# Whole-tile loads of K and V in a decode attention kernel: K tiles alternate between two overlapping places

## The chip, the core and the metric

The kernel runs on one core of a Trainium2 chip. The metric is the device time of one execution in microseconds. The profile's span, from the first to the last instruction, is 1.4 us shorter: 200.9 us in an execution of 202.28 us.

## What is computed

One token goes through a transformer layer: attention over a cache of 4096 positions with 32 heads of 128, then a gated feed-forward part. All tensors are bfloat16.

```
x  = A_x                                   # 1 x 640
q  = layernorm(x) @ wq                     # 640 -> 32 heads x 128
p  = softmax(q . k_cache / sqrt(128))      # 32 heads, 4096 positions each
o  = p @ v_cache                           # 32 x 128
h  = x + o @ wo                            # 4096 -> 640
g, u = layernorm(h) @ w_gate, layernorm(h) @ w_up     # 640 -> 1728
out  = h + (gelu(g) * u) @ w_down
```

Each head has its own keys and values, so no cache byte is used twice. K and V are 33.6 MB each; with the weights, 84.2 MB are read in all.

## The kernel before

**Tiles.** The work on the cache runs over four tiles (`j` from 0 to 3, `NG = 4`) of eight heads. A tile of K or V is 8.39 MB: on each of the 128 partitions 256 rows of 128 numbers, 64 KB in one piece of memory. Sixteen partitions share a head.

**Halves and quarters.** `k_all` has 64 KB per partition, one tile of K. It is loaded in two halves of 32 KB (`load_k(j, s)`, `HALF` = 128 rows), each with a landing event of its own. VectorE works on quarters of 64 rows: `mult(j, s, i)` (L393) multiplies quarter `i` of half `s` by the query into `prod[i]`. TensorE sums a product over groups of its 128 numbers by matmuls with the identity (`fold`, L369 and L167, 16 matmuls a quarter) into four PSUM banks. `total(j, s)` (L399) reduces what is left for both quarters of a half to 128 scores per partition, and ScalarE takes the exponential (L401). `block(j, s)` (L406) spreads the 128 probabilities into `p_bd[s]`, a block form that TensorE can multiply with V. There is no maximum subtraction.

**V.** `v_all` has 64 KB per partition, one tile of V, and holds wq before the first tile. `pv(s)` (L381) runs 32 matmuls of `p_bd[s]` with half `s` of V. The first three tiles of V come in one load each, the last in two. The next load of V waits for `pvs[j, 1]`, the end of the second half's matmuls.

**Order.** `Prog` keeps a list of operations for each engine, each with the events that it waits for; an engine works through its list in order. All big loads are issued by SyncE, whose list also runs in order: a load that waits holds up those behind it. VectorE's order for a tile is mult(0,0), mult(0,1), mult(1,0), total(0), mult(1,1), block(0), total(1), block(1). TensorE has a loop over the tiles with the steps f00, f01, f10, f11 (folds), p0, p1 (V matmuls) and h (sum over a head's partitions). In before, p0 waits for `blocks[j, 0]` and p1 for `blocks[j, 1]`. One-element GpSimd memsets of `spare` (L437) serve as a relay: each waits for the second half of V, and p1 waits for the memset.

**K's release.** The load of half `s` of tile `j + 1` waits for `mults[j, s, 1]`, the second product of that half.

**Tail.** After the last tile, wo goes into the first 40 KB of `k_all`, w_down into the 16.25 KB behind it, and w_gate and w_up into `v_all`. The loads of wo wait for the last product of tile 3; w_gate waits for the last V matmul, `pvs[3, 1]`; w_up and w_down are behind it in SyncE's list. TensorE then does the output projection (L486), a layer norm, gate and up (L516) and w_down (L539). Three nops stand on VectorE's list after the product `hm` (`idle("vector", 3)`).

Of the kernel before, what the change touches and what calls it, by code (L numbers as in the profile page):

```python
# [5 lines left out]
FP32 = mybir.dt.float32  # L6
BF16 = mybir.dt.bfloat16
ALU = mybir.AluOpType
ACTF = mybir.ActivationFunctionType
AX = mybir.AxisListType  # L10
# [3 lines left out]
DH = 128  # L14
# [6 lines left out]
NG = 4  # L21
# [158 lines left out]

def bass_sequential_preLN__gqa_block_cached__glu_gated_geglu__decode_kernel(nc, A_x, A_k_cache, A_v_cache, A_wq, A_wo, B_x, B_w_gate, B_w_up, B_w_down, out):
    sb = lambda name, shape, dt: nc.alloc_sbuf_tensor(name, shape, dt)
    k_all = sb("k_all", [128, 2 * 128 * DH], BF16)
    v_all = sb("v_all", [128, 256 * DH], BF16)
    prod = sb("prod", [128, 2, 64, DH], BF16)
    qb = sb("qb", [128, NG, DH], BF16)
    sc = sb("sc", [128, 128], FP32)
    pt = sb("pt", [128, 128], BF16)
    spare = sb("spare", [1, 1], FP32)
    own = sb("own", [128, 4], BF16)  # L190
    own8 = sb("own8", [128, 8], BF16)
    p_bd = sb("p_bd", [128, 2, 128, 8], BF16)
# [36 lines left out]
    ps_f = psum[:, 0:2048]  # L229
# [8 lines left out]
    wo_sb = k_all[:, 0:32 * D].rearrange("p (i n) -> p i n", i=32)  # L238
    tile3 = lambda ap: ap.rearrange("p (g d) -> p g d", d=DH)


    P = Prog(nc)
    V = lambda fn, *d: P.op("vector", fn, *d)
# [8 lines left out]
    mults, pvs = {}, {}  # L252
    landed = {}
    HALF = 128 * DH

    def load_k(j, s):
        src = A_k_cache[0, 8 * j:8 * j + 8, :, :].rearrange("h (p r) d -> (h p) (r d)", p=16)
        landed["K", j, s] = P.dma("sync", k_all[:, HALF * s:HALF * s + HALF], src[:, HALF * s:HALF * s + HALF],
                                  mults.get((j - 1, s, 1)))

    def load_v(j, lo, hi, *after, chan=None):
        src = A_v_cache[0, 8 * j:8 * j + 8, :, :].rearrange("h (p r) d -> (h p) (r d)", p=16)
        ev = P.dma("sync", v_all[:, HALF * lo:HALF * hi], src[:, HALF * lo:HALF * hi], *after, chan=chan)
        for i in range(lo, hi):
            landed["V", j, i] = ev

    load_k(0, 0)
    load_k(0, 1)


    c_xz = GP(lambda e: e.memset(xlnB[:, :, :], 0.0))
# [17 lines left out]
    c_own8 = GP(lambda e: e.affine_select(own8[:, :], own8[:, :], pattern=[[16, 8]], compare_op=ALU.is_ge,  # L289
                                          fill=0.0, base=15, channel_multiplier=-1), own1)  # L290
# [20 lines left out]
    def idle(eng, n):  # L311

        def fn(e):
            for _ in range(n):
                i = e.nop(hint="n", nofuse=True)
            return i
        return P.op(eng, fn)
# [37 lines left out]
    qd = T(q_proj, xl, d_wq)  # L355
    VM = lambda fn, *d: P.op("vector", fn, *d, chan="m")
    VR = lambda fn, *d: P.op("vector", fn, *d, chan="r")
    VB = lambda fn, *d: P.op("vector", fn, *d, chan="b")
    AS = lambda fn, *d: P.op("scalar", fn, *d, chan="s")
    GS = lambda fn, *d: P.op("gpsimd", fn, *d, chan="s")  # L360
    qa = VR(lambda e: e.tensor_copy(qb[:, :, :].rearrange("p g d -> p (g d)"), ps_q), qd)  # L361
    load_v(0, 0, 2, qd, chan="V")


    reds, exps, blocks, evs, folds, seen = {}, {}, {}, {}, {}, {}

    def half(e, i, s, first=True):
        for n in range(8):
# [4 lines left out]
    def fold(e, i):  # L373
        half(e, i, 0)
        return half(e, i, 1, False)

    def pv(e, s):
        vt = tile3(v_all[:, HALF * s:HALF * s + HALF])
        for b in range(32):
            a = 32 * (b % 4)  # L380
            i = e.matmul(ps_o[a:a + 32, :], p_bd[:, s, 4 * b:4 * b + 4, :].rearrange("p g j -> p (g j)"),  # L381
                         vt[:, 4 * b:4 * b + 4, :], start=(s == 0 and b < 4), stop=(s == 1 and b >= 28))
        return i

    def head_sum(e, at):
        for r in range(4):
            i = e.matmul(ps_a[:, bass.ds(at, 8)], po_sb[:, 128 * r:128 * r + 128], hs[:, r, :],  # L387
                         start=(r == 0), stop=(r == 3))
        return i

    def mult(j, s, i):
        kt = tile3(k_all[:, HALF * s:HALF * s + HALF])
        mults[j, s, i] = VM(lambda e: e.tensor_tensor(  # L393
            out=prod[:, i, :, :], in0=kt[:, 64 * i:64 * i + 64, :],
            in1=qb[:, j, :].unsqueeze(1).to_broadcast([128, 64, DH]), op=ALU.mult),
            landed["K", j, s], qa, folds.get((j, 0, i) if s else (j - 1, 1, i)))

    def total(j, s):
        reds[j, s] = VR(lambda e: e.reduce_sum(sc[:, :], ps_f.rearrange("p (g d) -> p g d", d=16), axis=AX.X), folds[j, s, 1],  # L399
                        exps.get((j, 0) if s else (j - 1, 1)))  # L400
        exps[j, s] = AS(lambda e: e.activation(pt[:, :], sc[:, :], ACTF.Exp, bias=zero_t[:, 0:1],  # L401
                                               scale=INV_SQRT_DH, accum_out=RS[:, 2 * j + s:2 * j + s + 1]), reds[j, s], c_eps,
                        blocks.get((j, 0) if s else (j - 1, 1)))

    def block(j, s):
        blocks[j, s] = VB(lambda e: e.tensor_tensor(  # L406
            out=p_bd[:, s, :, :], in0=pt[:, :].unsqueeze(2).to_broadcast([128, 128, 8]),
            in1=own8[:, :].unsqueeze(1).to_broadcast([128, 128, 8]), op=ALU.mult), exps[j, s], c_own8, pvs.get((j - 1, s)))

    T(None, c_idb, c_hs)  # L410
    lp = P.loop("tensor", range(NG), [
# [1 line left out]
        ("f01", lambda e, j: fold(e, 1), lambda j: [mults[j, 0, 1]], True),  # L413
        ("f10", lambda e, j: fold(e, 0), lambda j: [mults[j, 1, 0], reds[j, 0]], True),
        ("f11", lambda e, j: fold(e, 1), lambda j: [mults[j, 1, 1]], True),
        ("p0", lambda e, j: pv(e, 0), lambda j: [blocks[j, 0], landed["V", j, 0]], True),
        ("p1", lambda e, j: pv(e, 1), lambda j: [blocks[j, 1], seen[j]], True),
        ("h", lambda e, j: head_sum(e, j * 8), lambda j: [evs[j]], True)])
    for j in range(NG):
        for s in range(2):  # L420
# [3 lines left out]
    for j in range(NG):  # L424
        mult(j, 0, 0)
        mult(j, 0, 1)
        if j < NG - 1:
            load_k(j + 1, 0)
        mult(j, 1, 0)
        total(j, 0)  # L430
        mult(j, 1, 1)
        if j < NG - 1:
            load_k(j + 1, 1)
        block(j, 0)
        total(j, 1)
        block(j, 1)
        seen[j] = GS(lambda e: e.memset(spare[:, :], 0.0), landed["V", j, 1])  # L437
        if j < NG - 2:
            load_v(j + 1, 0, 2, pvs[j, 1], chan="V")
        elif j == NG - 2:  # L440
            load_v(j + 1, 0, 1, pvs[j, 1], chan="V")
            load_v(j + 1, 1, 2)
        evs[j] = AS(lambda e: e.copy(po_sb[:, :], ps_o), pvs[j, 1])  # L443

    rt = GP(lambda e: e.tensor_tensor(out=RT[:, :, :], in0=RS[:, :].unsqueeze(2).to_broadcast([128, 2 * NG, 8]),
                                     in1=own8[:, :].unsqueeze(1).to_broadcast([128, 2 * NG, 8]), op=ALU.mult), exps[NG - 1, 1])
    def z_sum(e):
        for s in range(2):
# [6 lines left out]
                                      in1=own[:, :].unsqueeze(1).to_broadcast([128, H, 4]), op=ALU.mult), at)  # L455
# [2 lines left out]
    ap = V(lambda e: e.tensor_copy(aP[:, :], ps_z[:, 32:64]), sp)  # L458


    d_wo = [P.dma("sync", wo_sb[:, i:i + 16, :], A_wo[:, :].rearrange("(p i) n -> p i n", i=32)[:, i:i + 16, :], mults[NG - 1, 1, 1])
            for i in (0, 16)]
    wg_sb = v_all[:, 0:5 * DF].rearrange("p (c n) -> p c n", c=5)
    wu_sb = v_all[:, 5 * DF:10 * DF].rearrange("p (c n) -> p c n", c=5)
# [7 lines left out]
    for o in (0, 1, 2, 3, 32, 33, 34, 35):  # L472
        lo = o - o % 32
# [55 lines left out]
    g6 = V(lambda e: e.tensor_mul(gu[:, :], g_t[:, :], t1[:, :]), g8)  # L529
    g9 = V(lambda e: e.tensor_mul(hm[:, :], gu[:, :], ps_u[:, 0:15]), g6, up)  # L530

    idle("vector", 3)

    def down(ms, qs=range(4)):
        def fn(e):
            for m in ms:
                for q in qs:
                    rows, wd = (128, wd_sb[:, m]) if m < 13 else (48, wd_lo[:, m - 13])
                    i = e.matmul(ps_d[32 * q:32 * q + 1, 0:160], hm[0:rows, m:m + 1],  # L539
                                 wd[0:rows, col[q]:col[q] + 160], start=False, stop=(m == 12))  # L540
            return i
        return fn
# [46 lines left out]
```

The softmax here doesn't subtract the row's maximum and nothing guards it: scores larger than these inputs give would overflow.

## Time and profile before

| | |
|---|---|
| time, median of 3 | 202.29 us (202.2 to 202.43) |
| span of the profiled execution | 200.9 us |
| read from HBM | 84.23 MB, 419 GB/s over the span |
| busy: TensorE matmul / VectorE / ScalarE | 115.3 / 103.6 / 9.4 us |
| 16 products of K (L393) | 4.42 us each |
| 8 reductions (L399) | 2.29 us each |
| 8 p_bd (L406) | 1.22 us each |
| TensorE clock granted, mean | 0.795 |

In the page, the row "DMA" gives for each of 40 equal slices of the span the mean busy share of the 16 transfer engines in tenths, and the row below what they moved. A line of the timeline is: start in us, length in us, engine, line, operation, output and inputs, how many, and in square brackets how long the engine stood idle before and what it waited for. "DMA" as a releaser means that a load landed. A line with SPq is SyncE issuing a transfer, not the transfer itself.

### The profile page before, as it was taken

What the parts mean: (1) busy time and instruction counts of PE and PEld (TensorE: products, weight loads), DVE (VectorE), ACT (ScalarE), POOL (GpSimd) and SP (SyncE); (2) the same over time, 40 slices, a digit from 0 to 9 for tenths busy, and PEclk for the clock granted to TensorE, in tenths of its full rate; (3) what the DMA queues carried; (4) which work ended last, traced back from release to release, by engine and by line L of the source; (5) the groups of instructions that cost most, each with busy time, mean ns of one, the idle gap of its engine ahead of it and who ended that gap; (6) DMA issues with size and microseconds to landing.
All of it is one profiled execution on the core that took longest, in us unless ns stands there. A gap on an engine that the chain in (4) does not pass through costs nothing.

```text
span 200.9 us, 2025 instructions
## 1 busy us (share of the span) xinstructions
PE 115.3 (57%) x982; PEld 30.4 (15%) x738; DVE 103.6 (52%) x56; ACT 9.4 (5%) x27; POOL 6.7 (3%) x36
## 2 busy tenths in 40 slices
PE   0108019667094296696605938566088496674675
PEld 0103000000032000001300000023000001474574
DVE  0200197994601969945149799420798965120320
ACT  2100000000001000000100000001000000100100
POOL 6500000000000000000000000000000000000000
PEclk9999856999858559579965899969669879955555
DMA  8999999999899999999999999899999999999992
GB/s 326 449 406 437 431 450 424 417 431 499 385 444 417 424 522 417 417 417 411 417 424 424 489 457 444 378 411 424 424 450 437 431 444 391 432 436 414 423 402 107
DMA packets 3275, 84.31 MB, mean 420 GB/s; under 512 B 387, under 2 KB 582, under 8 KB 966
## 3 DMA queue, kind: packets, MB, share of 16 engines
q1 hardware_dynamic: 3266, 84.23, 97.8%
q8 instruction: 4, 0.07, 0.1%
q14 instruction: 1, 0.01, 0.0%
q10 hardware_dynamic: 4, 0.00, 0.0%
HBM read 84.23 MB, written 0.00 MB: 419 GB/s over the span
## 4 chain that ended last, share of the span: by engine, by line
DMA 66%; DVE 22%; PE 11%; issue 0%; ACT 0%; SPq 0%; DVEq 0%
DMA k_all<-in_A_k_cache_dram 56%; DVE prod L393 18%; DMA v_all<-in_B_w_up_dram 10%; PE psum L167 7%; DVE sc L399 3%; PE psum L516 1%; PE psum L539 1%; PE psum L381 1%; DVE p_bd L406 1%; PE psum L369 1%; SPq L59 0%; ACT pt L401 0%; ACT out_row L555 0%; DVE hm L530 0%; DVEq L114 0%
## 5 line engine op out<-in xcount | busy, mean ns | idle before, releaser
L393 DVE TENSOR_TENSOR prod<-k_all,qb 128x8192 bf16<-128x8192 bf16 x16 | 70.4, 4421 | 38.0 <-DMA k_all<-in_A_k_cache_dram 33.1
L167 PE MATMUL psum<-prod,id_b 128*128 128x512 bf16 x240 | 66.0, 437 | 0.0
L369 PE MATMUL psum<-prod,id_b 128*128 128x512 bf16 x16 | 7.3, 454 | 45.3 <-DVE prod L393 31.5
L381 PE MATMUL psum<-v_all,p_bd 128*32 128x512 bf16 x256 | 19.4, 464 | 14.2 <-DMA v_all<-in_A_v_cache_dram 11.0
L399 DVE TENSOR_REDUCE sc<-psum 128x128 f32<-128x2048 f32 x8 | 18.3, 2288 | 13.3 <-PE psum L167 13.3
L369 PEld LDWEIGHTS psum<-prod,id_b 128*128 128x128 bf16 x16 | 1.6, 99 | 99.8 <-DVE prod L393 59.4
L381 PEld LDWEIGHTS psum<-v_all,p_bd 128*32 128x32 bf16 x256 | 7.5, 114 | 38.5 <-DMA v_all<-in_A_v_cache_dram 21.8
L406 DVE TENSOR_TENSOR p_bd<-pt,own 128x1024 bf16<-128x1024 bf16 x8 | 9.8, 1222 | 2.2 <-ACT pt L401 2.2
L401 ACT ACTIVATE pt<-sc,zero_t 128x128 bf16<-128x128 f32 x8 | 3.2, 402 | 135.9 <-DVE sc L399 135.9
L352 PE MATMUL psum<-v_all,xlnB 128*32 128x512 bf16 x40 | 4.5, 631 | 6.7 <-DMA v_all<-in_A_wq_dram 6.7
L486 PE MATMUL psum<-aP,k_all 128*128 128x1 bf16 x160 | 6.7, 178 | 2.7 <-DMA k_all<-in_A_wo_dram 2.7
L486 PEld LDWEIGHTS psum<-aP,k_all 128*128 128x128 bf16 x160 | 6.6, 131 | 2.8 <-DMA k_all<-in_A_wo_dram 2.8
L516 PE MATMUL psum<-hlnT,v_all 128*128 128x1 bf16 x150 | 5.5, 173 | 1.2 <-DMA v_all<-in_B_w_up_dram 1.2
L387 PE MATMUL psum<-hs,po_sb 128*128 128x8 f32 x32 | 4.2, 258 | 3.2 <-ACT po_sb L443 3.2
L437 POOL MEMSET spare<- 1x1 f32 x4 | 0.4, 88 | 162.8 <-DMA v_all<-in_A_v_cache_dram 162.8
L361 DVE CAST qb<-psum 128x512 bf16<-128x512 f32 x1 | 0.7, 692 | 9.7 <-PE psum L352 9.7
L516 PEld LDWEIGHTS psum<-hlnT,v_all 128*128 128x128 bf16 x150 | 5.3, 120 | 1.8 <-DMA v_all<-in_B_w_up_dram 1.3
L492 DVE COPY hT<-psum 128x5 f32<-128x5 f32 x1 | 0.2, 166 | 9.6 <-PE psum L486 9.6
L387 PEld LDWEIGHTS psum<-hs,po_sb 128*128 128x128 f32 x32 | 3.9, 191 | 5.1 <-issue 5.1
L323 PE MATMUL psum<-one_bf,x_row 1*128 1x1 bf16 x5 | 0.4, 177 | 7.1 <-DMA x_row<-in_A_x_dram 7.1
L326 DVE COPY xx<-psum 128x5 f32<-128x5 f32 x1 | 0.2, 165 | 7.5 <-PE psum L323 7.5
L443 ACT COPY po_sb<-psum 128x512 f32<-128x512 f32 x4 | 2.3, 585 | 22.3 <-PE psum L381 22.3
(71 smaller groups left out, 28.6 us busy)
## 6 DMA issues: line engine op xcount, KB each, us to landing
k_all<-in_A_k_cache_dram SPq DMA_DIRECT2D x8, 4096.0 KB, 29.1
v_all<-in_A_v_cache_dram SPq DMA_DIRECT2D x2, 4096.0 KB, 28.5
v_all<-in_A_wq_dram SPq DMA_DIRECT2D x1, 5120.0 KB, 15.2
k_all<-in_A_wo_dram SPq DMA_DIRECT2D x2, 2560.0 KB, 17.4
v_all<-in_B_w_gate_dram SPq DMA_DIRECT2D x1, 2160.0 KB, 15.0
v_all<-in_B_w_up_dram SPq DMA_DIRECT2D x1, 2160.0 KB, 19.8
k_all<-in_B_w_down_dram SPq DMA_DIRECT2D x1, 800.0 KB, 22.3
k_all<-in_B_w_down_dram SPq DMA_DIRECT2D x1, 640.0 KB, 20.9
```

The costliest lines, as they stand in the source:

```text
L167: built = e.matmul(out, lhsT, rhs, start=start, stop=stop)
L352: i = e.matmul(ps_q[32 * t:32 * t + 32, :], xlnB[:, c, 32 * a:32 * a + 32], wq_j[:, c, t, a, :, :], start=(c == 0 and a == 0), stop=(c == ...
L369: mm = held if n or not first else lambda e, *a, **k: e.matmul(*a, **k)
L381: i = e.matmul(ps_o[a:a + 32, :], p_bd[:, s, 4 * b:4 * b + 4, :].rearrange("p g j -> p (g j)"), vt[:, 4 * b:4 * b + 4, :], start=(s == 0 a ...
L387: i = e.matmul(ps_a[:, bass.ds(at, 8)], po_sb[:, 128 * r:128 * r + 128], hs[:, r, :], start=(r == 0), stop=(r == 3))
L393: mults[j, s, i] = VM(lambda e: e.tensor_tensor(out=prod[:, i, :, :], in0=kt[:, 64 * i:64 * i + 64, :], in1=qb[:, j, :].unsqueeze(1).to_br ...
L399: reds[j, s] = VR(lambda e: e.reduce_sum(sc[:, :], ps_f.rearrange("p (g d) -> p g d", d=16), axis=AX.X), folds[j, s, 1], exps.get((j, 0) i ...
L401: exps[j, s] = AS(lambda e: e.activation(pt[:, :], sc[:, :], ACTF.Exp, bias=zero_t[:, 0:1], scale=INV_SQRT_DH, accum_out=RS[:, 2 * j + s:2 ...
L406: blocks[j, s] = VB(lambda e: e.tensor_tensor(out=p_bd[:, s, :, :], in0=pt[:, :].unsqueeze(2).to_broadcast([128, 128, 8]), in1=own8[:, :]. ...
L443: evs[j] = AS(lambda e: e.copy(po_sb[:, :], ps_o), pvs[j, 1])
L486: r = e.matmul(ps_p[:, c:c + 1], wo_sb[:, i, c::5], aP[:, i:i + 1], start=False, stop=(i == 31), skip_group_check=True)
L516: i = e.matmul(ps[:, m:m + 1], ws, hlnT[:, c:c + 1], start=(c == 0 and m == 0), stop=(c == 4), skip_group_check=True)
```

## The change

K's whole tile comes in one load, and so does V's. `k_all` grows to 80 KB per partition. Even tiles of K lie at 0 to 64 KB, odd tiles at 16 to 80 KB (`K_AT`). The two places overlap in 48 KB, so the next tile can be loaded as soon as three of a tile's four quarters are used, if the one that lies outside the overlap is used last. For this, even tiles use their quarters in the order 2, 3, 1, 0 and odd tiles in the order 0, 1, 2, 3. The next load of K waits for the third product, `mults[j, 1, 0]`.

With the new order, the first pair of an even tile's products belongs to the second half of the positions: `half_of` puts its probabilities into the matching half of `p_bd`, and the second pair, which comes as quarters 1 and 0, is reduced in two instructions that swap them back. Both V steps now wait for the second `block` of the tile, and for the whole V tile; the relay on GpSimd is gone. The loads of wo wait only for tile 3's second product, since wo covers only its first two quarters. The three nops on VectorE near the end are taken out.

The aim is fewer and larger loads, with the next K tile requested once rather than in two steps.

```diff
-    k_all = sb("k_all", [128, 2 * 128 * DH], BF16)
+    k_all = sb("k_all", [128, 320 * DH], BF16)
...
-    def load_k(j, s):
+    K_AT = [0, 64 * DH, 0, 64 * DH]
+
+    def load_k(j):
...
-        landed["K", j, s] = P.dma("sync", k_all[:, HALF * s:HALF * s + HALF], src[:, HALF * s:HALF * s + HALF],
-                                  mults.get((j - 1, s, 1)))
+        landed["K", j] = P.dma("sync", k_all[:, K_AT[j]:K_AT[j] + 2 * HALF], src, mults.get((j - 1, 1, 0)))
...
+    def half_of(j, s):
+        return s if j % 2 else 1 - s
+
     def mult(j, s, i):
-        kt = tile3(k_all[:, HALF * s:HALF * s + HALF])
+        c = (2 * s + i) if j % 2 else (2 + i, 1 - i)[s]
+        kt = tile3(k_all[:, K_AT[j]:K_AT[j] + 2 * HALF])
...
-            out=prod[:, i, :, :], in0=kt[:, 64 * i:64 * i + 64, :],
+            out=prod[:, i, :, :], in0=kt[:, 64 * c:64 * c + 64, :],
...
-            landed["K", j, s], qa, folds.get((j, 0, i) if s else (j - 1, 1, i)))
+            landed["K", j], qa, folds.get((j, 0, i) if s else (j - 1, 1, i)))
...
+        if s and j % 2 == 0:
+            V(lambda e: e.reduce_sum(sc[:, 64:128], g16(0, 1024), axis=AX.X), folds[j, s, 1], free)
+            reds[j, s] = VR(lambda e: e.reduce_sum(sc[:, 0:64], g16(1024, 2048), axis=AX.X))
+        else:
+            reds[j, s] = VR(lambda e: e.reduce_sum(sc[:, :], g16(0, 2048), axis=AX.X), folds[j, s, 1], free)
...
-        ("p0", lambda e, j: pv(e, 0), lambda j: [blocks[j, 0], landed["V", j, 0]], True),
-        ("p1", lambda e, j: pv(e, 1), lambda j: [blocks[j, 1], seen[j]], True),
+        ("p0", lambda e, j: pv(e, 0), lambda j: [blocks[j, 1], landed["V", j]], True),
+        ("p1", lambda e, j: pv(e, 1), lambda j: [], True),
...
         mult(j, 0, 1)
+        mult(j, 1, 0)
         if j < NG - 1:
-            load_k(j + 1, 0)
-        mult(j, 1, 0)
+            load_k(j + 1)
         total(j, 0)
         mult(j, 1, 1)
-        if j < NG - 1:
-            load_k(j + 1, 1)
         block(j, 0)
         total(j, 1)
         block(j, 1)
-        seen[j] = GS(lambda e: e.memset(spare[:, :], 0.0), landed["V", j, 1])
-        if j < NG - 2:
-            load_v(j + 1, 0, 2, pvs[j, 1], chan="V")
-        elif j == NG - 2:
-            load_v(j + 1, 0, 1, pvs[j, 1], chan="V")
-            load_v(j + 1, 1, 2)
+        if j < NG - 1:
+            load_v(j + 1, pvs[j, 1])
...
-    d_wo = [P.dma("sync", wo_sb[:, i:i + 16, :], A_wo[:, :].rearrange("(p i) n -> p i n", i=32)[:, i:i + 16, :], mults[NG - 1, 1, 1])
+    d_wo = [P.dma("sync", wo_sb[:, i:i + 16, :], A_wo[:, :].rearrange("(p i) n -> p i n", i=32)[:, i:i + 16, :], mults[NG - 1, 0, 1])
...
-    idle("vector", 3)
-
```

More of the change, by code (lines that the diff above doesn't have):

```diff
@@ L188, in bass_sequential_preLN__gqa_block_cached__glu_gated_geglu__decode_kernel @@
     pt = sb("pt", [128, 128], BF16)
-    spare = sb("spare", [1, 1], FP32)
     own = sb("own", [128, 4], BF16)
@@ L254, in bass_sequential_preLN__gqa_block_cached__glu_gated_geglu__decode_kernel, with load_v @@
     HALF = 128 * DH
-    def load_k(j, s):
+    K_AT = [0, 64 * DH, 0, 64 * DH]
+    def load_k(j):
         src = A_k_cache[0, 8 * j:8 * j + 8, :, :].rearrange("h (p r) d -> (h p) (r d)", p=16)
-        landed["K", j, s] = P.dma("sync", k_all[:, HALF * s:HALF * s + HALF], src[:, HALF * s:HALF * s + HALF],
-                                  mults.get((j - 1, s, 1)))
-    def load_v(j, lo, hi, *after, chan=None):
+        landed["K", j] = P.dma("sync", k_all[:, K_AT[j]:K_AT[j] + 2 * HALF], src, mults.get((j - 1, 1, 0)))
+    def load_v(j, *after):
         src = A_v_cache[0, 8 * j:8 * j + 8, :, :].rearrange("h (p r) d -> (h p) (r d)", p=16)
[L263 to L268, printed above, removed]
+        landed["V", j] = P.dma("sync", v_all[:, 0:2 * HALF], src, *after, chan="V")
+    load_k(0)
     c_xz = GP(lambda e: e.memset(xlnB[:, :, :], 0.0))
@@ L361, in bass_sequential_preLN__gqa_block_cached__glu_gated_geglu__decode_kernel @@
     qa = VR(lambda e: e.tensor_copy(qb[:, :, :].rearrange("p g d -> p (g d)"), ps_q), qd)
-    load_v(0, 0, 2, qd, chan="V")
-    reds, exps, blocks, evs, folds, seen = {}, {}, {}, {}, {}, {}
+    load_v(0, qd)
+    reds, exps, blocks, evs, folds = {}, {}, {}, {}, {}
     def half(e, i, s, first=True):
@@ L389, in head_sum @@
         return i
+    def half_of(j, s):
+        return s if j % 2 else 1 - s
     def mult(j, s, i):
-        kt = tile3(k_all[:, HALF * s:HALF * s + HALF])
+        c = (2 * s + i) if j % 2 else (2 + i, 1 - i)[s]
+        kt = tile3(k_all[:, K_AT[j]:K_AT[j] + 2 * HALF])
         mults[j, s, i] = VM(lambda e: e.tensor_tensor(
-            out=prod[:, i, :, :], in0=kt[:, 64 * i:64 * i + 64, :],
+            out=prod[:, i, :, :], in0=kt[:, 64 * c:64 * c + 64, :],
             in1=qb[:, j, :].unsqueeze(1).to_broadcast([128, 64, DH]), op=ALU.mult),
-            landed["K", j, s], qa, folds.get((j, 0, i) if s else (j - 1, 1, i)))
+            landed["K", j], qa, folds.get((j, 0, i) if s else (j - 1, 1, i)))
     def total(j, s):
-        reds[j, s] = VR(lambda e: e.reduce_sum(sc[:, :], ps_f.rearrange("p (g d) -> p g d", d=16), axis=AX.X), folds[j, s, 1],
-                        exps.get((j, 0) if s else (j - 1, 1)))
+        free = exps.get((j, 0) if s else (j - 1, 1))
+        g16 = lambda lo, hi: ps_f[:, lo:hi].rearrange("p (g d) -> p g d", d=16)
+        if s and j % 2 == 0:
[3 more added lines that the diff above has]
+            reds[j, s] = VR(lambda e: e.reduce_sum(sc[:, :], g16(0, 2048), axis=AX.X), folds[j, s, 1], free)
         exps[j, s] = AS(lambda e: e.activation(pt[:, :], sc[:, :], ACTF.Exp, bias=zero_t[:, 0:1],
@@ L405, in block @@
     def block(j, s):
+        hf = half_of(j, s)
         blocks[j, s] = VB(lambda e: e.tensor_tensor(
-            out=p_bd[:, s, :, :], in0=pt[:, :].unsqueeze(2).to_broadcast([128, 128, 8]),
-            in1=own8[:, :].unsqueeze(1).to_broadcast([128, 128, 8]), op=ALU.mult), exps[j, s], c_own8, pvs.get((j - 1, s)))
+            out=p_bd[:, hf, :, :], in0=pt[:, :].unsqueeze(2).to_broadcast([128, 128, 8]),
+            in1=own8[:, :].unsqueeze(1).to_broadcast([128, 128, 8]), op=ALU.mult), exps[j, s], c_own8, pvs.get((j - 1, 1)))
     T(None, c_idb, c_hs)
```

## The prediction

> **What bounds the kernel now.** I read the page's DMA row and queue table first, because the kernel reads every byte of the two caches once.
>
> ```profile
> DMA  8999999999899999999999999899999999999992
> GB/s 326 449 406 437 431 450 424 417 431 499 385 444 417 424 522 417 417 417 411 417 424 424 489 457 444 378 411 424 424 450 437 431 444 391 432 436 414 423 402 107
> q1 hardware_dynamic: 3266, 84.23, 97.8%
> ```
>
> The transfer engines are busy from the first slice to the last but one. No compute engine passes 57% of the span. To see whether any gap is left, I take landing times from the timeline. The GpSimd memset of `spare` waits for nothing but a V landing, so its start is that landing:
>
> ```profile
> 54.92 0.09 POOL L437 MEMSET spare<- 1x1 f32 x1 [46.68 <-DMA v_all<-in_A_v_cache_dram]
> 93.70 0.09 POOL L437 MEMSET spare<- 1x1 f32 x1 [38.69 <-DMA v_all<-in_A_v_cache_dram]
> 132.48 0.09 POOL L437 MEMSET spare<- 1x1 f32 x1 [38.69 <-DMA v_all<-in_A_v_cache_dram]
> 171.34 0.09 POOL L437 MEMSET spare<- 1x1 f32 x1 [38.77 <-DMA v_all<-in_A_v_cache_dram]
> ```
>
> Steps of 38.78, 38.78 and 38.86 us, each with one K and one V tile between (16.78 MB): 432.6 GB/s, with no room for a gap. So the loads are an unbroken stream: wq, K0, V0, K1, V1, K2, V2, K3, V3, wo, the small pieces of w_down, w_gate, w_up, w_down.
>
> Next the chain of work that ended last, in order of time (start, length, what), from the last K half on:
>
> ```profile
> 124.58 27.28 DMA k_all<-in_A_k_cache_dram
> 151.85 0.02 issue
> 151.88 4.42 DVE prod L393
> ...
> 171.66 1.94 PE psum L381 x32
> 173.60 0.02 issue
> 173.61 0.34 SPq L59
> 173.95 0.04 issue
> 173.99 19.78 DMA v_all<-in_B_w_up_dram
> 193.77 0.05 issue
> 193.82 2.77 PE psum L516 x75
> ```
>
> The second half of K3 lands at 151.85. The arithmetic on it, up to the last probability-times-V matmul, ends at 173.60; that frees `v_all`, and w_gate and w_up are issued. w_up lands at 193.77 and the end follows 7.1 us later. The chain calls this one transfer of 19.78 us, but wo is still in front of it. The timeline of TensorE has its landing as the wait before the second half of the output projection:
>
> ```profile
> 183.53 3.36 PE L486 MATMUL psum<-aP,k_all 128*128 128x1 bf16 x80 [2.67 <-DMA k_all<-in_A_wo_dram]
> 193.82 2.75 PE L516 MATMUL psum<-hlnT,v_all 128*128 128x1 bf16 x75 [1.21 <-DMA v_all<-in_B_w_up_dram]
> ```
>
> From 183.53 to 193.77 is 10.24 us for w_gate and w_up (4.42 MB, 10.2 us at 432.6 GB/s): no gap there either. TensorE waits only 2.67 + 1.21 = 3.88 us for weights after 173.60. Without these waits the work after the last V matmul takes 200.9 - 173.60 - 3.88 = 23.4 us. **That is the whole slack of the tail.**
>
> Last, one tile of VectorE with its K at hand from the start, the third:
>
> ```profile
> 103.39 8.76 DVE L393 TENSOR_TENSOR prod<-k_all,qb 128x8192 bf16<-128x8192 bf16 x2 [7.15 <-DMA k_all<-in_A_k_cache_dram]
> 113.59 4.43 DVE L393 TENSOR_TENSOR prod<-k_all,qb 128x8192 bf16<-128x8192 bf16 x1 [1.44 <-PE psum L167]
> 117.93 2.28 DVE L399 TENSOR_REDUCE sc<-psum 128x128 f32<-128x2048 f32 x1
> 131.12 1.22 DVE L406 TENSOR_TENSOR p_bd<-pt,own 128x1024 bf16<-128x1024 bf16 x1 [0.56 <-ACT pt L401]
> 132.48 5.26 PE L381 MATMUL psum<-v_all,p_bd 128*32 128x512 bf16 x64 [4.25 <-DMA v_all<-in_A_v_cache_dram]
> ```
>
> From the first product to the end of the second p_bd are 132.34 - 103.39 = 28.95 us. The same stretch is 28.95 in tile 0, 31.64 in tile 1 (folds at half clock), 29.35 in tile 3.
>
> **What the Trainium skill says.** "DMA: Bandwidth & Descriptors", Specifications, puts the fabric's ceiling at 435 GB/s; the stream's 432.6 agrees and leaves 0.6%. Its section "Rules for kernel authors" asks for 128 partitions and at least 1 MiB per DMA; the loads already carry 4 and 8 MiB, and the trace shows no better rate for the larger: 9.67 us for the 4.19 MB of K2's first half (93.70 to 103.37), 19.49 us for the two V3 halves. Its section "Anatomy of one DMA" says that a semaphore wait is held on the issuing sequencer, not in the DMA engines, and that some 2 us of a DMA are fixed, most of it the write receipt. The trace: wq is issued at 0.0 and TensorE starts on it at 15.30; less 12.1 us for 5.24 MB, the fixed part is about 3.1 us on this queue. "TensorE: Matmul & The Clock Gate", "What's actually happening", says that the array falls to half clock after an idle window of about 3.4 us; the trace agrees: the V matmuls above, after 4.25 us idle, took 5.26 us for 64, and each batch of 32 in tile 3 at full clock 1.91.
>
> **The change, part by part.**
>
> *The rate.* K goes from eight loads to four, 512 of 3266 packets fewer. No gain at 432.6 of 435: the ceiling would give 84.23 MB × (1/432.6 - 1/435) = 1.1 us at most. I take 0; 1.1 is the bound.
>
> *First product.* It waits for the whole 8.39 MB tile, not the first half: 9.7 us later (4.19 MB). Whole tiles land at about 34.6, 74.3, 113.05 and 151.85.
>
> *Release of K.* The next load is issued after the third product: 10.2 to 10.8 us after the start (113.59 - 103.39; 75.42 - 64.61) plus 4.4, so 14.6 to 15.2. The V load in front lands 19.4 us after the K tile; to leave no gap the issue has to come 3.1 us before that, at 16.3. Fits by about 1 us: nothing.
>
> *Release of V.* Both V halves now wait for the second p_bd. In tiles 1 and 3 the first half ran under the last reduction; now 64 matmuls follow. Bounds: 2 × 1.91 = 3.8 us at full clock, 6.5 at half (tile 0: 64 in 6.47). I take tile 2's case, 5.26, for the idle time ahead is the same. Then V is issued 28.95 + 0.14 + 5.26 = 34.35 us after its K tile landed, and has to be by 38.78 - 3.1 = 35.7. Fits by 1.3 us; a tile like tile 1 (31.64) misses by 1.4.
>
> *Split reduction.* In tiles 0 and 2 one 2.29 us reduction becomes two of 1024 columns. The smallest reduction in the trace (ten columns) takes 0.17, so at most 0.2 more, within that spare. Not in tile 3.
>
> *The tail*, where the slack is smallest. Wo is released after tile 3's second product, near 161, ahead of V3's landing: hidden. The `spare` memsets and the three nops on VectorE (which waits 2.42 us for TensorE there): nothing. The rest:
> - from K3's landing to the last p_bd: now 171.52 - 151.88 = 19.64 us, because two products were done before the second half landed; then 28.95. **+9.3**
> - from the last p_bd to the last V matmul: now 173.60 - 171.52 = 2.08; then 0.14 + 5.26 = 5.40. **+3.3**
> - the waits for wo and w_up that this absorbs: **-3.9**
>
> Sum **+8.7**. The last V matmul ends at 151.87 + 28.95 + 5.40 = 186.2. Queued behind it on SyncE are w_gate, w_up and w_down. Wo lands at 183.5, so the stream has a gap of 186.2 + 3.1 - 183.5 = 5.8 us. But w_up lands at 186.2 + 3.1 + 10.2 = 199.5, and TensorE's own chain (projection, layer norm, gate) gets to it only 23.4 - 7.1 = 16.3 us after 186.2, at 202.5. So the arithmetic carries the end: 186.2 + 23.4 = 209.6 against 200.9. Time: 202.29 + 8.7 = **211.0**.
>
> **The rivals.**
> - *Gaps in mid-stream too.* If tile 1 again takes 31.64, the V2 load is 1.4 us late and all behind it shifts; a last tile with some half-clock folds adds about as much: 211.0 + 2.7 = 213.7. For it: spares of only 1 us. Against: two of the four tiles took 28.95. All ends together (31.64 and 6.5 in tile 3, and the gap) give 216.3.
> - *Only the load gap shows.* If TensorE runs the tail faster, with no idle time in it, w_up's landing sets the end: 199.5 + 7.1 = 206.6, or 202.29 + 5.8 = 208.1. Near it is the first theory with full clock: 28.3 (tile 3's first fold took 5.0 us, tile 2's 5.6) and 3.8 in place of 28.95 and 5.26 give 211.0 - 2.1 = 208.9.
> - *Slack swallows it, or larger packets pay: faster.* With the stream at the ceiling, and the last tile's extra 12.6 us absorbed, 202.29 - 1.1 = 201.2. Against it: the tail has 3.9 us of slack, and V's 64 KB packets run no faster now than K's 32 KB.
>
> **How the numbers follow.** First theory 0.66 at 211.0; mid-stream gaps 0.16 at 213.7; load gap only 0.11 at 208.1; faster 0.05 at 201.2; leftovers near no change 0.02. The range takes in the first three, from 208.0 (the load-gap case) to 214.5 (the gap case with part of the worst clock); beyond lie the last two cases and the worst sum, under 2 in 10. Slower: 0.66 + 0.16 + 0.11 = 0.93; same 0.02; faster 0.05.
>
> **What the profile would show.** First products at about 34.6, 74.3, 113.1 and 151.9; V landings still 38.8 apart (else: gaps). In the tail: the last p_bd near 180.8, w_gate issued near 186, a low DMA slice there, no wait of TensorE for wo or w_up, and the chain of waits running through K3, products, reductions, V matmuls and the projections. I am wrong if the whole K3 lands well before 151.85 (a faster stream), or if the stretch from its landing to the last p_bd is far from 29 us.

## The result, and the profile after

The changed kernel takes 213.93 us (median of 6 runs, 210.58 to 215.68), the kernel before 202.26 us. The ratio is 1.0505, 95% interval 1.0431 to 1.0578: slower. (Ratios, here and below, are not those of the medians: they come from the runs within 1.5% of the fastest of their kernel, here three of the six.) The profiled execution took 213.44 us, with a span of 212.2 us.

The page's DMA row, its queue line and the shares of the chain that ended last:

```profile
DMA  9899999999899989999999999999999979629980
GB/s 363 378 445 482 494 395 408 395 432 494 346 485 408 383 371 445 395 395 395 482 507 395 395 395 408 568 408 395 395 395 445 519 314 432 282 59 407 416 355 10
q1 hardware_dynamic: 2546, 84.23, 93.5%
DMA 51%; PE 27%; DVE 21%; issue 1%; ACT 1%; SPq 0%; DVEq 0%
```

The same bytes in fewer packets, but there is a hole: 282 and 59 GB/s in the two slices from 180 to 191 us. Up to there the transfers are nearly unbroken. TensorE's share of the chain has gone from 11% to 27%. The chain in order of time (start, length, what), from the last K tile on, shows where:

```profile
128.87 24.30 DMA k_all<-in_A_k_cache_dram
153.17 0.02 issue
153.19 4.44 DVE prod L394
...
181.16 1.24 DVE p_bd L413
182.40 0.12 issue
182.52 6.29 PE psum L378 x49
...
192.71 6.45 PE psum L487 x160
...
202.16 5.29 PE psum L517 x150
```

No load of weights is left in it. After K3 the end is set by arithmetic alone: products, folds, reductions, V matmuls, output projection, and gate and up in one unbroken run of 150 matmuls where before TensorE waited between the two.

VectorE's timeline has the first two products of each tile, and with them the landing of each whole K tile:

```profile
34.84 8.76 DVE L394 TENSOR_TENSOR prod<-k_all,qb 128x8192 bf16<-128x8192 bf16 x2 [14.00 <-DMA k_all<-in_A_k_cache_dram]
74.95 8.76 DVE L394 TENSOR_TENSOR prod<-k_all,qb 128x8192 bf16<-128x8192 bf16 x2 [8.52 <-DMA k_all<-in_A_k_cache_dram]
114.09 8.76 DVE L394 TENSOR_TENSOR prod<-k_all,qb 128x8192 bf16<-128x8192 bf16 x2 [8.67 <-DMA k_all<-in_A_k_cache_dram]
153.19 8.76 DVE L394 TENSOR_TENSOR prod<-k_all,qb 128x8192 bf16<-128x8192 bf16 x2 [9.96 <-DMA k_all<-in_A_k_cache_dram]
```

The last is 1.3 us later than an unbroken stream would have it (151.87). Half of that is there at the second tile (74.95, where the prediction had 74.3); the two steps after it are 39.1 us each in place of 38.8. In tile 0 the third fold ran at half clock (15 matmuls in 6.11 us, 3.40 at full clock), the V matmuls below took 6.21, and V1 was requested only 2.1 us before K1 landed:

```profile
49.98 0.33 SPq L59 DMA_DIRECT2D k_all<-in_A_k_cache_dram  x1
52.69 6.11 PE L167 MATMUL psum<-prod,id_b 128*128 128x512 bf16 x15
72.82 0.33 SPq L59 DMA_DIRECT2D v_all<-in_A_v_cache_dram  x1
```

The V matmuls in TensorE's timeline, all of them behind an idle gap of 4.3 us, and the request for w_gate that waits for the last of them:

```profile
66.56 6.21 PE L378 MATMUL psum<-v_all,p_bd 128*32 128x512 bf16 x64 [4.31 <-DVE p_bd L413]
105.56 5.32 PE L378 MATMUL psum<-v_all,p_bd 128*32 128x512 bf16 x64 [4.25 <-DVE p_bd L413]
143.37 5.32 PE L378 MATMUL psum<-v_all,p_bd 128*32 128x512 bf16 x64 [4.31 <-DVE p_bd L413]
182.52 6.26 PE L378 MATMUL psum<-v_all,p_bd 128*32 128x512 bf16 x64 [4.25 <-DVE p_bd L413]
...
188.82 0.34 SPq L59 DMA_DIRECT2D v_all<-in_B_w_gate_dram  x1
```

From 188.80, the end of the V matmuls, to the end of the span are 23.4 us. W_up was requested at 189.20. The page gives the time from there to its landing as the last figure:

```profile
v_all<-in_B_w_up_dram SPq DMA_DIRECT2D x1, 2160.0 KB, 13.7
```

So it landed near 202.9, and TensorE, busy with the gate from 202.09 on, got to it near 204.8.

### The profile page after: what moved, and what is told of

Read it like the earlier page. It is cut to its first block, busy times and chain, and to the rows that moved or that the text cites. A ratio compares the mean times of both kernels' runs of the same rounds, so it can differ in the third digit from the quotient of the medians.

```text
span 212.2 us, 2003 instructions
## 1 busy us (share of the span) xinstructions
PE 121.0 (57%) x982; PEld 31.9 (15%) x738; DVE 103.8 (49%) x58; ACT 9.4 (4%) x27; POOL 7.4 (3%) x32
## 3 DMA queue, kind: packets, MB, share of 16 engines
q1 hardware_dynamic: 2546, 84.23, 93.5%
## 4 chain that ended last, share of the span: by engine, by line
DMA 51%; PE 27%; DVE 21%; issue 1%; ACT 1%; SPq 0%; DVEq 0%
DMA k_all<-in_A_k_cache_dram 51%; DVE prod L394 17%; PE psum L167 14%; PE psum L487 3%; PE psum L378 3%; PE psum L517 2%; DVE sc L406 2%; PE psum L366 1%; PE psum L538 1%; DVE p_bd L413 1%; PE psum L384 0%; DVE hX L501 0%; PE psum L497 0%; PE psum L327 0%; ACT po_sb L444 0%
## 5 line engine op out<-in xcount | busy, mean ns | idle before, releaser
L167 PE MATMUL psum<-prod,id_b 128*128 128x512 bf16 x240 | 68.4, 449 | 0.0
L366 PE MATMUL psum<-prod,id_b 128*128 128x512 bf16 x16 | 7.5, 466 | 51.1 <-DVE prod L394 37.7
L378 PE MATMUL psum<-v_all,p_bd 128*32 128x512 bf16 x256 | 23.1, 541 | 17.1 <-DVE p_bd L413 17.1
L406 DVE TENSOR_REDUCE sc<-psum 128x128 f32<-128x2048 f32 x6 | 13.7, 2287 | 6.7 <-PE psum L167 6.7
L378 PEld LDWEIGHTS psum<-v_all,p_bd 128*32 128x32 bf16 x256 | 9.1, 130 | 43.9 <-issue 42.4
L446 POOL TENSOR_TENSOR RT<-RS,own 128x64 f32<-128x64 f32 x1 | 1.3, 1324 | 172.9 <-ACT pt L407 172.9
L403 DVE TENSOR_REDUCE sc<-psum 128x64 f32<-128x1024 f32 x2 | 2.4, 1224 | 7.2 <-PE psum L167 7.2
## 6 DMA issues: line engine op xcount, KB each, us to landing
k_all<-in_A_wo_dram SPq DMA_DIRECT2D x2, 2560.0 KB, 19.5
```

The source lines that it names most:

```text
L167: built = e.matmul(out, lhsT, rhs, start=start, stop=stop)
L366: mm = held if n or not first else lambda e, *a, **k: e.matmul(*a, **k)
L403: V(lambda e: e.reduce_sum(sc[:, 64:128], g16(0, 1024), axis=AX.X), folds[j, s, 1], free)
L406: reds[j, s] = VR(lambda e: e.reduce_sum(sc[:, :], g16(0, 2048), axis=AX.X), folds[j, s, 1], free)
```

## The experiments

The theory is that of the prediction: a whole tile has to land before its first product, nothing hides that in the last tile, and the V matmuls behind the last p_bd add to it. The rivals: the loads themselves (larger packets, a single request, late requests) cost the time.

### Two loads for each K tile

```diff
-        landed["K", j] = P.dma("sync", k_all[:, K_AT[j]:K_AT[j] + 2 * HALF], src, mults.get((j - 1, 1, 0)))
+        if True:
+            for n in range(2):
+                h = n if j % 2 else 1 - n
+                landed["K", j, n] = P.dma("sync", k_all[:, K_AT[j] + HALF * h:K_AT[j] + HALF * h + HALF],
+                                          src[:, HALF * h:HALF * h + HALF], mults.get((j - 1, 1, 0)))
+            return
+        ev = P.dma("sync", k_all[:, K_AT[j]:K_AT[j] + 2 * HALF], src, mults.get((j - 1, 1, 0)))
+        landed["K", j, 0] = landed["K", j, 1] = ev
...
-            landed["K", j], qa, folds.get((j, 0, i) if s else (j - 1, 1, i)))
+            landed["K", j, s], qa, folds.get((j, 0, i) if s else (j - 1, 1, i)))
```

> The changed kernel with each K tile in two loads of 32 KB per partition, issued one behind the other at the same event (the third product of the tile before), the half that is used first in front, each half with its own landing event. Whole-tile theory (the first product of a tile waits 9.7 us longer, and in the last tile nothing hides that): the last p_bd falls from 29.2 us after K3 is complete to about 19.7, the V matmuls end near 178, and 178 + 23.4 is 201.4, close to the load stream's own end at 200.9; time 202.3 to 203.5. Rival, fewer and later requests (the third product releases K, the last V matmul releases V, so the stream has gaps) with the first product's start of little weight: over 208.

Measured: 202.60 us (202.13 to 204.95), ratio 1.0051, interval 1.0026 to 1.0076. Nearly the whole loss is gone, but the 20 runs fall into two groups: 11 took 202.1 to 202.7, 9 took 203.9 to 205.0. The profiled one (202.28) is of the first group. The last tile and the tail, from the timelines of VectorE and TensorE:

```profile
142.16 8.76 DVE L401 TENSOR_TENSOR prod<-k_all,qb 128x8192 bf16<-128x8192 bf16 x2 [7.25 <-DMA k_all<-in_A_k_cache_dram]
152.25 4.42 DVE L401 TENSOR_TENSOR prod<-k_all,qb 128x8192 bf16<-128x8192 bf16 x1 [1.33 <-PE psum L167]
...
171.24 5.15 PE L385 MATMUL psum<-v_all,p_bd 128*32 128x512 bf16 x64 [4.36 <-DMA v_all<-in_A_v_cache_dram]
193.72 2.74 PE L524 MATMUL psum<-hlnT,v_all 128*128 128x1 bf16 x75 [1.21 <-DMA v_all<-in_B_w_up_dram]
```

The first product is back at 142.16, and two products are done at 150.9, before the second half is in (near 151.85). The V matmuls wait for V3's landing; in the changed kernel V3 was in long before them (by 12 us in the execution that shows V's landings, below). W_up's landing is again the last wait. The V matmuls still come all at the end in this kernel, but they end at 176.4, early enough for w_gate.

### Two loads, but both waited for

This kernel keeps the two loads and makes every product of a tile wait for the second. (GpSimd memsets that show V's landings are added.)

```diff
-            landed["K", j, s], qa, folds.get((j, 0, i) if s else (j - 1, 1, i)))
+            landed["K", j, 1], qa, folds.get((j, 0, i) if s else (j - 1, 1, i)))
```

> K in two loads of 32 KB per partition as in the kernel with halved K loads, but every product of a tile waits until both halves have landed. Theory that the wait for the whole tile counts and not the size of the load: as slow as the changed kernel, 211 to 216, first product of the last tile near 152 to 153. Rival, the larger packets or the single request count: near 203.

Measured: 214.06 us (212.54 to 217.19), ratio 1.0559, interval 1.0527 to 1.0591. With the same two loads, the time is that of the changed kernel. So it is the wait that costs, not the size or number of K's loads. The first product of the last tile came later than expected in the profiled execution, which at 217.19 us is the slowest of the four:

```profile
154.52 8.76 DVE L402 TENSOR_TENSOR prod<-k_all,qb 128x8192 bf16<-128x8192 bf16 x2 [10.53 <-DMA k_all<-in_A_k_cache_dram]
```

### Two loads for the last K tile alone

The edit is that of the first experiment with `j == NG - 1` in place of `True`.

> The changed kernel with the last K tile alone in two loads; tiles 0 to 2 stay in one load. Whole-tile theory, in which it is the last tile that counts: K3 is complete at about 153.2 as now, the last p_bd comes 19.7 us later, the stream's end sets the time: 202.3 plus the 1.3 us that the first three tiles lose, 203.6 (up to 204.5). Rival, the loss comes from requests in mid-stream: still above 210.

Measured: 204.85 us (204.06 to 205.96), ratio 1.0115, interval 1.0087 to 1.0143. So the last tile is worth about three quarters of the loss (9.1 of 11.7 us by the medians). The time is 1.25 us above what was expected. The profiled execution is the slowest of the four (205.96). Its rows of the transfers have a hole (218 GB/s in the slice from 107.4 to 112.5). Below them are SyncE's request for V2, the first products of tiles 2 and 3, and the last load in the chain that ended last:

```profile
DMA  9999999999999999999995999999999997999992
GB/s 337 424 469 410 410 410 525 461 436 410 413 410 410 410 423 474 500 423 410 436 410 218 410 410 410 410 410 410 448 551 436 410 410 345 436 440 409 429 392 86
...
112.67 0.33 SPq L59 DMA_DIRECT2D v_all<-in_A_v_cache_dram  x1
...
113.46 8.76 DVE L401 TENSOR_TENSOR prod<-k_all,qb 128x8192 bf16<-128x8192 bf16 x2 [7.24 <-DMA k_all<-in_A_k_cache_dram]
144.23 8.76 DVE L401 TENSOR_TENSOR prod<-k_all,qb 128x8192 bf16<-128x8192 bf16 x2 [1.83 <-DMA k_all<-in_A_k_cache_dram]
...
182.83 19.33 DMA k_all<-in_B_w_down_dram
```

V2 was requested 0.8 us before K2 had landed. V2 and the first half of K3 then took 30.77 us; at the stream's 432.6 GB/s these 12.58 MB take 29.1. A late request costs. It explains only part of what this execution is above 203.6, though: K3 was complete at 153.9, 0.7 us later than was assumed. The rest lies behind that landing, where the last load in the chain is w_down (202.15), and no longer w_up. Why it came that late is not shown.

### The first V matmuls early

V comes in two loads, swapped for even tiles, so that the first p_bd goes with the first half of `v_all`; `p_bd` is indexed by `s`.

```diff
...
-        ("p0", lambda e, j: pv(e, 0), lambda j: [blocks[j, 1], landed["V", j]], True),
-        ("p1", lambda e, j: pv(e, 1), lambda j: [], True),
+        ("p0", lambda e, j: pv(e, 0), lambda j: [blocks[j, 0], landed["V", j]], True),
+        ("p1", lambda e, j: pv(e, 1), lambda j: [blocks[j, 1]], True),
```

> The changed kernel with the first 32 V matmuls released by the first p_bd of a tile again: V comes in two loads of 32 KB per partition, and for even tiles the halves are swapped in v_all, so that the half used first fits the first pair of K quarters; K stays in one load. Theory that the arithmetic carries the end: in the last tile the stretch from the last p_bd to the last V matmul falls from 6.4 us to about 2.1, all of it shows: 213.9 - 4.3 = 209.6 (207.5 to 211.5). Rival, the gap in the loads carries the end: w_gate is issued 4.3 us earlier as well, so the time falls by up to the same amount, but then the projections wait for weights; no such wait is expected by the first theory.

Measured: 210.20 us (209.16 to 210.91), ratio 1.0389, interval 1.0371 to 1.0406: 3.7 less than the changed kernel. In the last tile of the profiled execution, the fastest of the five:

```profile
176.59 1.91 PE L381 MATMUL psum<-v_all,p_bd 128*32 128x512 bf16 x32
...
180.83 3.59 PE L381 MATMUL psum<-v_all,p_bd 128*32 128x512 bf16 x32 [2.33 <-DVE p_bd L416]
```

Half of the matmuls now lie under the last reduction. The other half ran at half clock (3.59 for 32, granted clock 0.50), so the stretch behind the last p_bd fell from 6.42 to 3.68 us, 2.7 less and not 4.3. Another 1.3 us came from mid-stream: with V requested earlier, K3 was complete at 151.91. TensorE waited neither for wo nor for w_up, so the arithmetic still carries the end.

### TensorE kept at work before the V matmuls

```diff
+    def keep(e):
+        for n in range(16):
+            i = e.matmul(ps_s, id_b[:, :], ones_b[:, 0:1].to_broadcast([128, 512]), start=True, stop=True)
+        return i
...
+        ("w", lambda e, j: keep(e), lambda j: [], False),
         ("p0", lambda e, j: pv(e, 0), lambda j: [blocks[j, 1], landed["V", j]], True),
```

> The changed kernel with 16 further matmuls (identity by ones, into a PSUM bank that nobody reads) in TensorE's loop between the last fold and the first V matmul, where TensorE now stands idle for 4.25 us. Theory that the V matmuls are slow because TensorE comes to them idle: the 64 take 3.8 to 4.2 us instead of 5.3 to 6.3, time 213.9 - 2.2 = 211.7. Rival, the granted clock does not follow this idle time: unchanged at 213.9, or later if the added matmuls run at half clock (16 x 0.43 = 6.8 us, 2.6 more than the gap).

Measured: 210.06 us (209.86 to 210.87), ratio 1.0399, interval 1.0377 to 1.0421. More work on TensorE makes the kernel 3.9 us faster:

```profile
176.57 3.65 PE L376 MATMUL psum<-ones_b,id_b 128*128 128x512 bf16 x16
180.98 3.64 PE L383 MATMUL psum<-v_all,p_bd 128*32 128x512 bf16 x64 [0.76 <-DVE p_bd L418]
```

The 64 V matmuls take 3.64 us in place of 6.26. That is 2.6 of the gain. Mid-stream gave 1.5 more: the V requests came earlier, and K3 was complete at 151.66 in place of 153.17. The tail gave back 0.6, with a pause of 0.5 in the output projection. V1's request came 5.4 us earlier, and only about half of that is the V matmuls; the other half is that neither fold of the second half of tile 0 ran at half clock here. The four runs lie within 1.0 us, the six of the changed kernel within 5.1.

### Reading V's landings in the changed kernel

One-element GpSimd memsets, one for each V load, are put back for this.

> The changed kernel with one-element GpSimd memsets that wait for each V load, so that V's landings can be read in the timeline; nothing else is changed. Theory that the 1.3 us lost before the last tile come from requests made too late: a V tile that was requested less than about 3.3 us before the K tile in front of it landed takes more than 19.4 us from that landing; one requested earlier takes 19.4. Rival, K in 64 KB packets is itself slower: every K tile takes about 0.35 us more than 19.4 whenever it was requested. Time 211 to 216 as before.

One execution, 215.89 us. GpSimd's timeline:

```profile
54.20 0.09 POOL L443 MEMSET spare<- 1x1 f32 x1 [45.96 <-DMA v_all<-in_A_v_cache_dram]
93.53 0.09 POOL L443 MEMSET spare<- 1x1 f32 x1 [39.25 <-DMA v_all<-in_A_v_cache_dram]
133.71 0.09 POOL L443 MEMSET spare<- 1x1 f32 x1 [40.09 <-DMA v_all<-in_A_v_cache_dram]
172.52 0.09 POOL L443 MEMSET spare<- 1x1 f32 x1 [38.72 <-DMA v_all<-in_A_v_cache_dram]
```

With the requests on SyncE and the first products of this execution (74.16, 113.19, 153.06) this gives, for each load of 8.39 MB, how long before the landing of the load in front it was requested, and how long after that landing its own came:

| load | requested ahead, us | took, us |
|---|---|---|
| K1 | 4.7 | 19.9 |
| V1 | 4.8 | 19.4 |
| K2 | 3.9 | 19.6 |
| V2 | 3.2 | 20.5 |
| K3 | 5.8 | 19.3 |
| V3 | 5.3 | 19.5 |

The latest request, V2's, took 1.1 us more. K3, in 64 KB packets, ran at the full rate, so the packets are not slower. There is no sharp edge: V2 was requested 3.2 to 3.3 us ahead in the changed kernel and in the one with warm matmuls too, and there the step from K2 to K3 was 39.1 and 38.8 us, nearly or fully the rate of before. In the kernel in which both halves are waited for, requests 4.0 to 4.1 us ahead were followed by landings 2.3 (K1), 0.9 (K2) and 0.4 us (V2) late.

The single packets in the traces show the gap itself. In the changed kernel all 16 transfer engines work until 72.4; then they run dry, down to one or two near 73.5. V1 was issued at 72.82, its packets start from 73.8 on, and all engines work again at 74.5. K1's landing let VectorE start only at 74.95, some 2.5 us after the engines had begun to run dry. In the observed execution it is 2.2 us for K2, and V2's packets start 1.3 us after the request.

### V requested late

Based on the kernel with halved K loads: each V load after the first waits for the second product of its own tile.

```diff
         mult(j, 0, 1)
+        if j:
+            load_v(j, pvs[j - 1, 1], mults[j, 0, 1])
         mult(j, 1, 0)
...
-        if j < NG - 1:
-            load_v(j + 1, pvs[j, 1])
```

> The kernel with halved K loads, with each V load after the first held back until the second product of the next tile is done; that is about 0.9 us before the second K half lands. Theory of the late request (a load has to be issued some 3.1 us before the load in front of it lands): a gap of 3.1 - 0.9 = 2.2 us at each of three V loads, V landings 41 us apart, time 202.3 + 6.6 = 208.9. Rival, a request that is made while the load in front is still running costs nothing: 202.3. The kernel in which only K3 was halved suggests something between: a V2 request 0.8 us ahead there, and 1.7 us lost.

Measured: 208.69 us (208.45 to 208.93), ratio 1.0317, interval 1.0302 to 1.0333. The V landings, again by memsets on GpSimd:

```profile
54.85 0.09 POOL L452 MEMSET spare<- 1x1 f32 x1 [46.61 <-DMA v_all<-in_A_v_cache_dram]
95.08 0.09 POOL L452 MEMSET spare<- 1x1 f32 x1 [40.15 <-DMA v_all<-in_A_v_cache_dram]
135.74 0.09 POOL L452 MEMSET spare<- 1x1 f32 x1 [40.57 <-DMA v_all<-in_A_v_cache_dram]
176.11 0.09 POOL L452 MEMSET spare<- 1x1 f32 x1 [40.28 <-DMA v_all<-in_A_v_cache_dram]
```

The steps are 40.2, 40.7 and 40.4 us, 1.4 to 1.9 above 38.8: some 4.8 in all, where 6.6 were expected. A further 1.8 us were lost between V3 and w_up (24.3 us, before 22.4); no transfer engine stands idle there, and the cause stays open. So the total fits better than its parts.

### Both repairs together

Halved K loads and early V matmuls in one kernel, again with memsets that show V's landings.

> The changed kernel with K in two loads (the half used first in front) and the first 32 V matmuls released by the first p_bd, both repairs together; what is left of the change is the 80 KB area, the order of the quarters and the release of K after the third product. All theories: the load stream sets the end again, V landings 38.78 us apart, time 202.2 (202.0 to 202.6). Theory that the upper runs of the kernel with halved K loads alone (to 204.9) are those in which V matmuls at half clock end too late: they go away here.

Measured: 202.47 us (202.29 to 202.72), ratio 1.0012, interval 1.0005 to 1.0018. The upper runs of the kernel with halved K loads (to 204.95) are gone, as they should be if late V matmuls caused them; no trace of such a run was taken, so that is argued, not shown. What is left of the change, the 80 KB area and the release after the third product, brings nothing. The 0.2 us above the kernel before lie in the stream: from V0's landing to V3's are 116.60 us, before 116.42. Why is not shown; this kernel has more packets, 3698. No version tried beats the kernel before.

## Why the prediction was right

It forecast 211.0 us in 208.0 to 214.5; 213.93 were measured. It was right in what sets the end: the wait for the whole last tile, then its products and V matmuls, then arithmetic that no load holds up. Its size was low by 2.9 us. The median lies on the figure of the rival with gaps in mid-stream too (213.7), which the range was meant to take in, and two of the six runs lie above the range. The profiled span can be set against the sum of 209.6, term by term:

- **First product after the whole tile.** Right, and shown by the pair of kernels with two loads, 202.60 with each half used as it lands and 214.06 with both waited for. From K3's landing to the end of the last p_bd are 182.38 - 153.19 = 29.19 us; 28.95 was taken. +0.2. That it came so near is in part luck: in the execution with V's landings observed, with K3 there at 153.06, the same stretch took 31.72 us, because two folds ran at half clock for longer (6.3 and 6.6 us in place of 5.1 and 5.3).
- **V matmuls behind the last p_bd.** Right in kind. The stretch took 188.80 - 182.38 = 6.42 us where 5.40 was taken. +1.0. The prediction had taken tile 2's case between the bounds of 3.8 and 6.5; in the last tile the upper bound nearly came true, at half clock almost to the end.
- **Slack absorbed, then 23.4 us of arithmetic.** Right: 212.2 - 188.8 = 23.4, with no wait of TensorE for wo or w_up. W_up landed 1.9 us before TensorE got to it, where the prediction had 3.0. The low DMA slice is there.
- **Release of K and V without a gap.** This step failed: it cost 1.3 us, K3 being there at 153.19 and not 151.87. The release of V was said to fit by 1.3 us, with 34.35 us from a K tile's landing to the request. In tile 0 they were 38.0 (72.82 - 34.84): the last p_bd came after 31.6 us and not 28.95, because of the fold at half clock, which tile 0 did not have before, and the V matmuls took 6.21 us and not 5.26. The prediction had this case for tile 1, as its rival. K's release, said to fit by 1 us, did not quite fit either: K1 was requested 15.1 us after K0 landed, as forecast, and landed 0.7 us late; why is not shown. The required 3.1 us, taken from the first load of the kernel, were too few. The engines run dry 2.2 to 2.5 us before a landing is seen, and new packets start 1.0 to 1.3 us after a request, so some 3.2 to 3.8 us are needed at the least (an estimate from the traces above, which does not explain the losses seen with 4.0 us). The kernel with late V requests shows that such a gap costs time, and the kernel with warm matmuls that it goes away when V is requested earlier.

The terms are stretches of one execution that follow each other, so the misses have to add up, and they do: 0.2 + 1.0 + 1.3 = 2.5, and 209.6 + 2.5 is the measured span within 0.1 us.

- **Rate.** Right: no gain from 720 packets fewer on the queue, and no loss. (The prediction counted 512. The runs show 144 for each tile that comes in two loads and not one: 2546, 2690, 3122 and 3698 with none, one, four and eight such tiles. Five make 720.) In the kernel with warm matmuls, with K and V in 64 KB packets, the last two K tiles landed 38.8 us apart, as V did before. The pair of times by which the prediction compared sizes was no comparison: V3 came in two loads before, so both figures are of 4 MiB loads. In the observed execution V3 came in one load and took 19.5 us, as its two halves did before.
- **The rivals.** Mid-stream gaps came true in addition to the first theory, and nearly in the size forecast (2.5 us in all, 2.7 forecast), but in other places: K1's and V1's loads in place of V2's, and the V matmuls of the last tile in place of its folds. That only the load gap shows did not: TensorE found w_up landed, here and in each kernel that waits for a whole last tile. Nothing swallowed the loss.
- **Wo released earlier, nops and split reduction at nothing.** Not tried alone. The two parts of the reduction took 1.23 and 1.22 us in place of 2.29, within the bound given. The kernel with both repairs contains all three and is 0.2 us from the kernel before.

## What to carry to other kernels

Here transfers filled the whole span at one rate for both sizes, so merging loads had nothing to win, and each landing event that went took overlap with it: in mid-stream there was nearly room, but the last tile had 3.9 us of slack for 12.6 us of added work. Work out for the last tile what runs from its landing to the end, and keep there the smallest piece that work can start on. Look also at how far ahead of the landing in front each load is requested; in these traces every request less than 3 us ahead lost time, some of those 3.2 to 4.1 us ahead did, and those more than 5 us ahead did not.

## What the runs showed of the hardware that was not expected

- Idle time of TensorE became time: 64 V matmuls took 3.64 us right behind other matmuls, and 5.1 to 6.3 after 4.3 us idle. "TensorE: Matmul & The Clock Gate" in the Trainium skill, under "What's actually happening", has half clock after an idle window of some 3.4 us, which agrees. But less idle time can do it: in the kernel with early V matmuls the second batch of the last tile ran at half clock after only 2.33 us idle, while those of the other three tiles, after 2.33 to 2.40 us, ran at full clock.
- Once arithmetic carried the end, single runs differed by 5.1 us; the kernel before, bound by its loads, stayed within 0.6 (202.08 to 202.62) in all its runs. Two traces with K3 at the same time (153.19 and 153.06) have spans of 212.2 and 214.6 us, and the difference is in the clock of the last tile's folds. That the whole spread comes from the clock is argued, not shown.
- A request that reached the queue 0.8 us before the load in front landed cost 1.7 us, one at 3.2 us cost 1.1. That is one trace; in the changed kernel V2, also 3.2 us ahead, cost at most 0.3. The packets show why late requests cost: the engines began to run dry 2.2 to 2.5 us before the landing was seen.
- GpSimd's only product near the end (RT, 128x64) took 1.32 us after a wait of about 11 us or more, and 0.29 when a memset had just run ahead of it. It was off the path here.
